# Identity products in spare PSUM columns while TensorE waits in the first batch's attention

## The chip, the cores and the metric

The kernel runs on one core of a Trainium2 chip. A core has a matrix engine (TensorE, PE in the rows below, with a weight loader PEld beside it), VectorE (DVE), ScalarE (ACT), GpSimd (POOL) and SyncE (SP), which issues the transfers. Each engine takes its instructions in the order of the program, and semaphores make one wait for another. The metric is the device time of one execution in microseconds.

## The reference

Pooled attention over 8 batches of 8 heads feeds a gated feed-forward layer.

```python
def _attn_ref(q, k, v) -> np.ndarray:
    B, H, S, D = q.shape                      # 8, 8, 576, 64
    pool = 8
    Sp = S // pool
    scale = 1.0 / np.sqrt(D)
    k_p = k.reshape(B, H, Sp, pool, D).mean(axis=3)
    v_p = v.reshape(B, H, Sp, pool, D).mean(axis=3)
    scores = scale * np.matmul(q, k_p.transpose(0, 1, 3, 2))
    scores = scores - np.max(scores, axis=-1, keepdims=True)
    attn = np.exp(scores)
    attn = attn / (np.sum(attn, axis=-1, keepdims=True) + 1e-09)
    return np.matmul(attn, v_p).astype(np.float32)
...
def _moe_ref(x, w_gate, w_val, w_out, rms_g) -> np.ndarray:   # x: 4608 x 512, hidden width 1536
    rms = np.sqrt(np.mean(x * x, axis=-1, keepdims=True) + 1e-06)
    xn = x / rms * rms_g
    g = xn @ w_gate
    silu = g * (1.0 / (1.0 + np.exp(-g)))
    val = xn @ w_val
    return (silu * val @ w_out).astype(np.float32)
```

## The kernel before

The attention works on one batch and one pair of heads at a time: batch 0 has the pairs 0 to 3. The feed-forward layer works on blocks of 512 tokens. Its first block needs all four pairs of batch 0 and most of its weights, which VectorE, ScalarE and GpSimd first split into a high and a low part. From the third block on, the products are formed by a scheme with seven products in place of eight. So the program starts with a short stretch in which all engines prepare, some 60 us, and then TensorE has feed-forward products to the end.

The order of the work is written out by hand in the long string `ORDER` (line 52). Each word of it is a step, and `run` (line 1109) calls the steps in that order; an engine's own order is the order in which the steps issue to it. Digits behind a colon name the PSUM banks that a step takes. A bank holds 128 x 512 numbers; there are eight, and a step that takes a bank waits for the readers of what stood in it. A leading `_` marks a step of batch 0, of batch 1's first pairs or of the first feed-forward block.

The steps that matter here, with batch b, pair p and half h or u (`_M021` is batch 0, pair 2, half 1):

- `K`, `V`: VectorE pools the keys and the values (lines 410, 419).
- `S` (`s_heads`, line 470): TensorE's scores, ten products into two banks, of which 5 x 72 = 360 columns are used. `M` takes the maxima and `U` subtracts them on VectorE (lines 428, 448), `E` and `O` make exponentials on ScalarE (lines 441, 453), `N` normalises on GpSimd (line 468).
- `T` (`s_pt`, line 525): TensorE transposes the weights, `C` and `D` copy them out on VectorE and ScalarE (lines 542, 544). Step `T` with half 2 uses 256 columns of its bank.
- `A` (`s_av`, line 545): weights times values, 288 columns. `Y`, `x` and `Z` read the result on ScalarE (lines 583, 1017, 590; `Z` squares it), `y` on VectorE (line 1023).
- `P` (`s_tokens`, line 637): TensorE sums the squares by products with a column of ones (line 652, tile psr). `p`, `r`, `s` make the reciprocal root, `B` spreads it (line 676, tile psb), `m` are the first gate products (line 1049, tile psg).
- `z` (`warm`, line 1170): products of the identity with itself. There is one such step, `_zg`, the first of all: 16 products.

An fp32 product shows as two MATMUL rows in the trace, a transpose as one.

Of the kernel before, what the change touches and what calls it, by code (L numbers as in the profile page):

```python
# [53 lines left out]
_k01 _O021 _K01 _f _k03 _v03 _V03 _I021 _K03 _R000 _O001 _q01 _I001 _h5 _N000 _N001 _S01:10 _M010 _k10 _M011 _U011
_E020 _N021 _R020 _K10/1 _N020 _q03 _S03:56 _M030 _E010 _l1 _R010 _W5 _M031 _N010 _q10 _O011 _T000:3 _I011 _N011 _E030
_v02 _D000 _l0 _a1/1 _a0/0 _V02 _R030 _S10:04 _M100 _l2 _U031 _T020:2 _E100 _l3/1 _b1 _c1 _N030 _T022:3 _D022 _b0 _d1
_O031 _c0 _h1 _W1 _a2 _R100 _T001:7 _d0 _T002:1 _D001 _D002 _T030:6 _D030 _T011 _I031 _N031 _M101 _a3/1 _T021:5 _D021
_C011 _E101 _N100 _T010:3 _T031 _v00 _V00 _A001:7/0 _Z01 _Y001 _x01 _D020 _b3 _b2 _c3 _c2 _d2 _h0 _y01 _T012:1 _W0
_A000:5 _Z00 _h2 _W2 _D012 _T032:6 _D010 _v01 _A020:4 _k11 _d3 _h3 _l4 _P00:2 _V01 _C032 _w3 _R101 _A021:1 _v10 _x20
_y20 _A010:3 _x00 _y00 _V10/0 _m000:7 _K11/1 _Y021 _x21 _y21 _Z21 _m010:6 _D031 _l7/0 _a7/1 _b7 _c7 _a4 _Z10 _ld/1 _l6  # L60
_ad/0 _m002 _b4 _Z20 _bd _A011:5 _Y011 _Z11 _d7 _x11 _A030 _x30 _Z30 _cd _c4 _x10 _dd _A031:4 _Z31 _P01 _P02 _P03 _a6
_hd _m012 _N101 _d4 _l9/0 _p _T100:1/1 _T101:2 _q11 _y30 _x31 _b6 _k12 _Wd _y11 _r0 _h7 _D101 _y31 _s0 _B00:5 _h4 _y10
_m011 _m001 _m013 _D100 _a9/0 _m003 _n _W4 _m100:5 Wt0/1 _l8 _Y031 _c6 _d6 _W7 _v11 _a8 _T102 _u0 _G0 _h6 _A100:1/1
_S11:27 _b9 _C102 _c9 _d9 _M110 _h9 _m102 _E110 _b8 _m110 _m112 _M111 _F0 _w9 _m101 _W6 _c8 _i0/1 _L0 Wf00 _d8 _lb/0
_R110 _m111 _K12/1 _A101:4 _ab/1 _X101 _bb _B01:6 _h8 _H01 _cb _m103 _u1 wf01 _db Wf02 _E111 _w8 _G1 _m113 _F1 wh03/0
Wl03 _la _X100 _hb _Wb _lf/0 Wf03 ws03 _e2:0 _o0:7564 _aa _g2:3 _i1/1 _ba _ca _L1 wh02/1 _o1 wl02 _af/0 _u2 _G2 _R111
_bf _cf _F2 _N110 _Q10 wd0 _i2/1 _T110:2/1 _D110 _df _hf _Wf _da _j2 _ha _g3:1 _lc _q12 _e3:0 wh01/0 _V11/0 _u3 _G3
_wa ws02 _o2 _N111 _F3 _ac _bc _cc _dc _k13 _i3/0 _lh/0 _ah/1 _hc _g4 _T112:1 _bh _D112 _j3 _T111:3 _le _D111 _e4:0
_ch _u4 _dh _hh wl01 ws01 Wt1/0 wh04/0 _ae Wl04 _Wc Wf10 _S12:32 _lg _Wh Wf11 Wf12 wf13 _be _M120 _M121 ws04 _G4 _F4
wh11/1 wl11 _ce _de _A110:1 _v20/1 _V20/1 _Y110 ws11 _o3 _A111:1 wh13/0 wd1 _i4/0 Wt2/1 _E120 _g5:0 wh14/1 _R120 Wl14  # L70
ws14 Wf20 _li Wl13 _L4 ws13 _ag _o4 _bg _e6 _he _We Wf21 _u5 _cg _E121 _R121 _dg wf22 _N121 wh12/1 Wl12 _e5:2 ws12 _G5
_Y111 _T121:1/1 Wf23 _F5 _i5/0 wh23/0 _v12 _j5 _N120 _D121 Wl23 wh21/1 Wl21 _q13 _K13/1 _T122 _ai _bi _ll/0 _hg ws23
ws21 _Wg _g6 _u6 _V12/0 _D122 _lk _k20 _v13 _o5 _G6 wh22/1 _F6 _i6/1 _ci _S13:10 _M130 _T120:3 _di wh24/0 Wl24 _D120
_j6 wl22 _M131 _g7 _u7 _hi ws22 _e7 _ak _o6 _K20/1 _bk _ck _G7 _F7 ws24 _E130 _dk _A121:3 _al/1 _bl _cl _ln/1 _an/0
_bn _cn _dl _i7/1 _R130 _dn _E131 _R131 _N131 _A120:2 _Y120 _hn _Wn _j7 _Y121 _g8:1 _u8 _V13/0 _G8 _wi _N130 wd4 _e8:0
_F8 _hl _wl _lj/0 _aj/0 _bj _cj _lm/1 _am/1 _bm _dj _T131:1/1 _o7 _D131 _hk _T130 _D130 _q20 sc20:21 wd2 _Q11/0 _cm
_T132 _D132 _dm _Wk _hj _A130:3 _Y130 Wt3/1 Wf30 _A131 _Y131 Wf31 lv21/0 mx201/1 sb201 _hm _Wj _wm _J11 mx200/1 lk21
# [1132 lines left out]
```

## Time and profile before

| | us |
|---|---|
| median of 3 runs | 975.91 (975.13 to 976.47) |
| the profiled execution, its own time | 976.88 |
| its span, first to last instruction | 975.1 |
| TensorE busy | 947.5 (97%) |
| VectorE, ScalarE, GpSimd busy | 704.2, 492.9, 490.4 |

The share of TensorE is that of the whole span. The stretch that the change touches is the first 60 us, where TensorE waits at places and where its granted clock changes several times; a view by short windows and the engines' timelines show that stretch.

### The profile page before, as it was taken

Reading aid. Unit: us, or ns where it says so; the run is one execution under the profiler, and the core shown is the slowest. Engines: PE = TensorE matmul, PEld = TensorE weight load, DVE = VectorE, ACT = ScalarE, POOL = GpSimd, SP = SyncE. Lnnn points to the kernel's source line nnn. Section 1 sums busy time; section 2 is a strip of 40 time slices with the busy share of each in tenths; the row PEclk is TensorE's granted clock in tenths of the full one; section 3 lists DMA queues with packets and bytes.
Section 4 is the critical chain, followed back from the end, with each engine's and each line's share of the span. In section 5 each row is a group of like instructions: output and inputs, shape, how many; then the busy total and the mean of one; then the engine's idle time right before and its main releaser. Section 6 shows DMA issues by size and latency. Waiting matters only on the chain.

```text
span 975.1 us, 14181 instructions
## 1 busy us (share of the span) xinstructions
PE 947.5 (97%) x4670; PEld 752.2 (77%) x4670; DVE 704.2 (72%) x1134; ACT 492.9 (51%) x929; POOL 490.4 (50%) x618
## 2 busy tenths in 40 slices
PE   7799999999999999999999999999999999999997
PEld 6577677777777877877877777877877778888885
DVE  6989898978787888778787877755565884433333
ACT  5876675645555647555455456242543642213332
POOL 3355637222322324433455788432296894445785
PEclk7789999999999999999999999999999999999999
DMA  9537774665766569878887776768686465767646
GB/s 300 183 137 273 225 247 157 215 204 178 240 204 204 171 182 267 251 231 274 253 248 255 202 253 195 243 184 263 217 257 212 155 219 173 229 189 232 205 141 204
DMA packets 142296, 211.41 MB, mean 217 GB/s; under 512 B 12240, under 2 KB 78288, under 8 KB 140944
## 3 DMA queue, kind: packets, MB, share of 16 engines
q1 hardware_dynamic: 142224, 210.52, 68.8%
...
HBM read 154.24 MB, written 56.23 MB: 216 GB/s over the span
## 4 chain that ended last, share of the span: by engine, by line
PE 76%; DMA 5%; DVE 5%; POOL 5%; ACT 3%; issue 2%; SPq 1%; DVEq 0%; ACTq 0%; POOLq 0%
PE pxy L895 30%; PE psg L1059 15%; PE pf L975 15%; PE po L1093 7%; PE psx L560 3%; PE pss L478 3%; POOL w L292 2%; DMA pt<-rows 1%; DMA ring<-vs 1%; POOL xp L292 1%; POOL hl L292 1%; DMA ring<-vB 1%; DVE wt L326 1%; PE psr L652 1%; DVE wt L330 1%
## 5 line engine op out<-in xcount | busy, mean ns | idle before, releaser
L895 PE MATMUL pxy<-xp,wp 128*128 128x512 f32 x1512 | 361.1, 391 | 1.5 <-ACT o L1104 0.7
L895 PEld LDWEIGHTS pxy<-xp,wp 128*128 128x128 f32 x1512 | 282.3, 188 | 65.3 <-issue 2.5
L975 PE MATMUL pf<-fp,ring 128*128 128x512 f32 x756 | 189.8, 393 | 3.1 <-DMA ring<-vB 1.6
L1059 PE MATMUL psg<-xh,w 128*128 128x512 f32 x544 | 171.2, 396 | 1.4 <-DVE prob L495 1.0
L975 PEld LDWEIGHTS pf<-fp,ring 128*128 128x128 f32 x756 | 139.6, 188 | 39.6 <-DMA ring<-vs 3.9
L1059 PEld LDWEIGHTS psg<-xh,w 128*128 128x128 f32 x544 | 101.2, 189 | 26.5 <-DVE prob L495 1.4
L1059 PE MATMUL psg<-xl,w 128*128 128x512 f32 x272 | 106.7, 392 | 0.0
L292 POOL TENSOR_TENSOR hl<-act,hh 128x256 fp32r<-128x256 f32 x58 | 49.8, 878 | 111.5 <-ACT hh L1075 102.6
L292 POOL TENSOR_TENSOR fp<-fs,fp 128x256 fp32r<-128x256 f32 x108 | 81.1, 778 | 41.7 <-ACT fp L948 37.9
L292 POOL TENSOR_TENSOR fp<-act,fp 128x256 fp32r<-128x256 f32 x72 | 55.1, 786 | 83.1 <-ACT fp L948 81.8
L1093 PE MATMUL po<-w,hh 128*128 128x512 f32 x288 | 72.9, 390 | 0.0
L292 POOL TENSOR_TENSOR w<-wt,w 128x256 fp32r<-128x256 f32 x50 | 48.7, 1000 | 45.7 <-ACT w L344 45.7
L1093 PEld LDWEIGHTS po<-w,hh 128*128 128x128 f32 x288 | 54.1, 188 | 11.6
L292 POOL TENSOR_TENSOR fp<-hb,fp 128x256 fp32r<-128x256 f32 x68 | 54.5, 828 | 13.9 <-ACT fp L948 13.9
L1059 PEld LDWEIGHTS psg<-xl,w 128*128 128x128 f32 x272 | 51.4, 189 | 11.1
L1154 ACT COPY hb<-pxy 128x512 f32<-128x512 f32 x36 | 21.0, 586 | 72.7 <-PE pxy L895 72.7
L1161 DVE TENSOR_TENSOR u<-u,pxy 128x512 f32<-128x512 f32 x36 | 24.7, 685 | 38.0 <-PE pxy L895 37.8
L948 ACT CAST fp<-act 128x512 fp32r<-128x512 f32 x36 | 22.2, 619 | 58.5 <-DVE act L1162 49.3
L948 ACT CAST fp<-fs 128x512 fp32r<-128x512 f32 x54 | 33.0, 618 | 34.3 <-POOL fs L292 16.7
L1155 DVE TENSOR_TENSOR u<-hb,pxy 128x512 f32<-128x512 f32 x36 | 24.6, 684 | 33.3 <-PE pxy L895 19.7
L292 POOL TENSOR_TENSOR fs<-act,hb 128x256 f32<-128x256 f32 x32 | 23.4, 752 | 50.0 <-DVE act L1162 28.0
L1158 DVE TENSOR_TENSOR hb<-u,pxy 128x512 f32<-128x512 f32 x36 | 24.7, 686 | 29.0 <-PE pxy L895 28.1
...
## 6 DMA issues: line engine op xcount, KB each, us to landing
wp<-sum SPq DMA_DIRECT2D x144, 256.0 KB
wp<-blocks SPq DMA_DIRECT2D x108, 256.0 KB
...
```

The costliest lines, as they stand in the source:

```text
L292: getattr(eng, op)(*(x[..., o:o + step] for x in (out, a, b)))
L478: nc.tensor.matmul(s["ps", h][:, t * SP:(t + 1) * SP], s["q"][r, o:o + P], s["pk"][r, :], start=True, stop=True)
L560: nc.tensor.matmul(ps[r, :n], s["pv"][:, r], x, start=True, stop=True)
L895: nc.tensor.matmul(ps[:, :NB], w[:, a, c, :], x[:, b, c, :], start=j == 0 and not more, stop=j == len(todo) - 1, skip_group_check=more)
L948: nc.scalar.copy(y[:, 0], f_source(i, k, j))
L975: nc.tensor.matmul(ps[c], w[:, a, c * P:(c + 1) * P], x[:, b], start=j == 0 and n == 0 and not more, stop=j == HALF - 1 and n == 2, skip_g ...
L1059: nc.tensor.matmul(ps[:, :NB], w[:, c, cols], x[c], start=(j == 0), stop=(j == len(todo) - 1))
L1093: nc.tensor.matmul(po[i][t], x[i, f][:, t * P:(t + 1) * P], w, start=(f == 0 and k == 0), stop=(f == NF - 1 and k == 2))
L1154: cp=lambda i, f: S_.copy(later(i, f), st["XY", i, f, 0]),
L1155: u2=lambda i, f: V.tensor_add(u2(i, f), later(i, f), st["XY", i, f, 1]),
L1158: c2=lambda i, f: V.tensor_sub(later(i, f), u3(i, f), st["XY", i, f, 4]),
L1161: v1=lambda i, f: V.tensor_add(u2(i, f), u2(i, f), st["XY", i, f, 5]),
```

## The change

Five steps `_z` with 10, 4, 9, 7 and 3 products are put between the steps of batch 0, and the first one grows from 16 products to 22 (`_zg` to `_zm`, the count is in base 36) and takes bank 1 in place of bank 6. All other steps keep their order. The new ones have no bank of their own: the list `spare` holds the last 128 columns of a bank that `S`, `T` (half 2) or `A` has just taken, which those steps leave unused.

```diff
@@ ORDER, the lines with a new step @@
-_zg:6 _q00 _q02 _l5/0 _k00 _K00 _S00:16 _a5/0 _b5 _c5 _k02 _K02 _S02:24 _M001 _M000 _U001 _E000 _d5 _M021 _M020 _U021
...
+_zm:1 _q00 _q02 _l5/0 _k00 _K00 _S00:16 _a5/0 _b5 _c5 _k02 _K02 _S02:24 _M001 _M000 _U001 _E000 _d5 _M021 _M020 _U021
+_k01 _O021 _K01 _f _k03 _v03 _V03 _I021 _K03 _R000 _O001 _q01 _I001 _h5 _N000 _N001 _za _S01:10 _M010 _k10 _M011 _U011
+_E020 _N021 _R020 _K10/1 _N020 _q03 _S03:56 _M030 _E010 _l1 _R010 _W5 _M031 _N010 _q10 _O011 _z4 _T000:3 _I011 _N011
...
@@ s_heads @@
         for h in (0, 1):
             s["ps", h] = bank(0, f"pss{b}_{p}_{h}")
+        spare[:] = [s["ps", 1][:, 512 - P:]]
@@ s_pt @@
         ps = s["pst", h] = bank(0, f"pst{b}_{p}_{h}")
+        if h == 2:
+            spare[:] = [ps[:, 512 - P:]]
@@ s_av @@
         ps = s["psx", u] = bank(0, f"psx{b}_{p}_{u}")
+        spare[:] = [ps[:, 512 - P:]]
@@ warm @@
-        ps = bank(0, "warm")
+        ps = spare[0] if spare else bank(0, "warm")[:, 512 - P:]
         for _ in range(n):
-            nc.tensor.matmul(ps[:, :P], ident, ident, start=True, stop=True)
+            nc.tensor.matmul(ps, ident, ident, start=True, stop=True)
```

`_z9` stands between `_T010` and `_T031`, `_z7` between `_D010 _v01` and `_A020`, `_z3` between `_dd` and `_A031`.

TensorE between the scores of pair 2 and those of pair 1, before. The names are tile, batch, pair and half; in brackets stand the engines or transfer queues whose semaphore the row waits for.

```order
L478 MATMUL pss0_2_0_138<-own2_136,main2_111 128x72
L478 MATMUL pss0_2_1_139<-own2_136,main2_111 128x72
L478 MATMUL pss0_1_0_190<-own1_168,main1_164 128x72 [waits DMAHW1_49,DVE_49,Activation_49]
L478 MATMUL pss0_1_1_191<-own1_168,main1_164 128x72
L478 MATMUL pss0_1_0_190<-own1_168,main1_164 128x72
```

The same place after the change:

```order
L480 MATMUL pss0_2_0_144<-own2_142,main2_117 128x72
L480 MATMUL pss0_2_1_145<-own2_142,main2_117 128x72
L1179 MATMUL pss0_2_1_145<-ident_69 128x128 [waits DVE_49]
L1179 MATMUL pss0_2_1_145<-ident_69 128x128 x9
L480 MATMUL pss0_1_0_206<-own1_174,main1_170 128x72 [waits DMAHW1_49,DVE_49,Activation_49]
L480 MATMUL pss0_1_1_207<-own1_174,main1_170 128x72
```

Ten identity products now stand ahead of pair 1's scores, and the first waits for VectorE: its semaphore value is that of `_U021`, the last instruction of VectorE that reads the tile pss0_2_1.

TensorE between the last scores of pair 3 and the first of batch 1, before:

```order
L478 MATMUL pss0_3_1_221<-own3_176,main3_171 128x72
L536 MATMUL pst0_0_0_250<-ident_69,main0_108 72x128 [waits Pool_49]
L536 MATMUL pst0_0_0_250<-ident_69,main0_108 72x128 x3
L478 MATMUL pss1_0_0_275<-pk1_0_216,q1_0_247 128x72 [waits DMAHW5_49,DVE_49,PE_49]
L478 MATMUL pss1_0_1_276<-pk1_0_216,q1_0_247 128x72
```

And after:

```order
L480 MATMUL pss0_3_1_237<-own3_182,main3_177 128x72
L1179 MATMUL pss0_3_1_237<-ident_69 128x128 [waits DVE_49]
L1179 MATMUL pss0_3_1_237<-ident_69 128x128 x3
L540 MATMUL pst0_0_0_270<-ident_69,main0_114 72x128 [waits Pool_49]
L540 MATMUL pst0_0_0_270<-ident_69,main0_114 72x128 x3
L480 MATMUL pss1_0_0_295<-pk1_0_232,q1_0_263 128x72 [waits DMAHW5_49,PE_49]
```

Four products and a wait for VectorE (for `_M031`, the last reader of pss0_3_1 that is issued ahead of them) now stand ahead of the transposes `_T000` and of batch 1's scores `_S10`.

TensorE around the last product of weights and values of batch 0, before:

```order
L560 MATMUL psx0_1_1_490<-own1_168 64x288 x2
L560 MATMUL psx0_3_0_498<-own3_176 64x288 [waits Activation_49]
L560 MATMUL psx0_3_0_498<-own3_176 64x288
L560 MATMUL psx0_3_1_508<-own3_176 64x288 [waits PE_49,Activation_49]
L560 MATMUL psx0_3_1_508<-own3_176 64x288
L652 MATMUL psr0_428<-one_74,own1_168 128x1 x2
```

And after:

```order
L565 MATMUL psx0_1_1_526<-own1_174 64x288 x2
L565 MATMUL psx0_3_0_534<-own3_182 64x288 [waits Activation_49]
L565 MATMUL psx0_3_0_534<-own3_182 64x288
L1179 MATMUL psx0_3_0_534<-ident_69 128x128 [waits Activation_49]
L1179 MATMUL psx0_3_0_534<-ident_69 128x128 x2
L565 MATMUL psx0_3_1_547<-own3_182 64x288 [waits PE_49]
L565 MATMUL psx0_3_1_547<-own3_182 64x288
L657 MATMUL psr0_464<-one_74,own1_174 128x1 x5
```

Three products stand ahead of `_A031`. They wait for ScalarE's `_Z30`, the square that reads psx0_3_0; before, `_A031` waited for the older square `_Z20`, which had read the bank that `_A031` takes.

## Rows read from the trace of the kernel before

**Rows 1.** The head of the profile's page and its line of busy times.

```profile
span 975.1 us, 14181 instructions
PE 947.5 (97%) x4670; PEld 752.2 (77%) x4670; DVE 704.2 (72%) x1134; ACT 492.9 (51%) x929; POOL 490.4 (50%) x618
```

**Rows 2.** The chain of work that ended last, in order of time, around the sums of squares: start us, us, what.

```profile
40.52 0.37 DVE xl L1023
...
41.22 0.57 ACT own L542
...
44.30 0.31 ACT own L590
...
44.65 0.71 PE psx L560 x4
45.36 6.01 PE psr L652 x30
51.37 1.49 PE psg L1049 x3
52.86 1.71 PE pst L536 x8
54.57 1.84 PE psb L676 x10
```

**Rows 3.** TensorE's timeline: start us, us, engine, line, operation, tile, count, and in brackets the idle time before it with what ended it.

```profile
1.47 5.46 PE L1174 MATMUL warm<-ident 128*128 128x128 f32 x32 [1.47 <-POOL ident masks.py:199]
...
10.69 1.51 PE L478 MATMUL pss<-own,main 64*128 64x72 f32 x20 [0.38 <-DVE own L410]
14.63 4.79 PE L478 MATMUL pss<-own,main 64*128 64x72 f32 x40 [2.43 <-DVE own L410]
19.35 1.07 PE L536 MATMUL pst<-ident,main 128*72 128x128 f32 x4
20.34 2.41 PE L478 MATMUL pss<-pk,q 64*128 64x72 f32 x20
...
26.19 1.50 PE L536 MATMUL pst<-ident,main 128*72 128x128 f32 x12 [0.28 <-ACT prob L441]
29.83 0.63 PE L536 MATMUL pst<-ident,main 128*72 128x128 f32 x4 [2.13 <-POOL main L468]
...
34.07 0.71 PE L560 MATMUL psx<-own 72*64 72x288 f32 x4 [1.65 <-ACT own L542]
...
42.64 1.19 PE L560 MATMUL psx<-own 72*64 72x288 f32 x8
44.65 0.71 PE L560 MATMUL psx<-own 72*64 72x288 f32 x4 [0.82 <-ACT own L590]
45.29 6.08 PE L652 MATMUL psr<-one,own 128*128 128x1 f32 x30
```

**Rows 4.** Windows of 1 us in which the granted clock changes: the window, its length, busy us (and instructions) of PE, PEld, DVE, ACT and POOL, then the clock (1.00 is 2.4 GHz, 0.50 is 1.2 GHz, between them the mean of both), the DMA share and GB/s.

```profile
11.00:12.00 1.00, 1.00 (x20) 0.99 (x16) 1.00 (x4) 0.42 (x2) 0.00 (x0) 0.86 1.04 363
...
25.00:26.00 1.00, 0.91 (x7) 0.58 (x5) 1.00 (x4) 1.00 (x8) 0.00 (x0) 0.82 0.47 122
...
35.00:36.00 1.00, 1.00 (x8) 1.00 (x9) 1.00 (x2) 1.00 (x3) 1.00 (x2) 0.80 0.00 0
...
42.00:43.00 1.00, 1.00 (x6) 0.38 (x7) 0.58 (x2) 1.00 (x2) 0.00 (x0) 0.78 0.02 8
...
45.00:46.00 1.00, 1.00 (x10) 0.71 (x6) 1.00 (x3) 1.00 (x5) 0.00 (x0) 0.92 0.00 0
...
56.00:57.00 1.00, 1.00 (x7) 0.87 (x6) 0.97 (x2) 1.00 (x3) 0.79 (x1) 0.96 0.00 0
```

**Rows 5.** Windows that count the rows of line 1174 alone (the opening identity products); a row that began before the window counts too. Columns: window, length, busy us (and rows) of PE and PEld, clock, DMA share, GB/s.

```profile
2.00:4.50 2.50, 2.50 (x14) 2.50 (x13) 1.00 0.90 267
5.00:6.50 1.50, 1.50 (x16) 1.50 (x15) 1.00 0.98 321
2.00:2.01 0.01, 0.01 (x2) 0.01 (x1) 1.00 0.11 4
...
5.00:5.01 0.01, 0.01 (x3) 0.01 (x2) 1.00 5.72 1638
```

**Rows 6.** VectorE's timeline: `_U021`, then `_M010` with `_M011`, `_M031`, and the first maxima of batch 1, `_M100`.

```profile
13.35 0.52 DVE L448 TENSOR_TENSOR main<-pss,early 128x360 f32<-128x360 f32 x1
...
17.59 0.94 DVE L428 TENSOR_REDUCE early<-pss 128x5 f32<-128x360 f32 x2
...
20.45 0.49 DVE L428 TENSOR_REDUCE early<-pss 128x5 f32<-128x360 f32 x1
...
22.92 0.49 DVE L428 TENSOR_REDUCE early<-pss 128x5 f32<-128x360 f32 x1
...
30.28 1.12 DVE L322 TENSOR_SCALAR wt<-wt 128x512 uint32<-128x512 uint32 x2 [0.21 <-ACT wt L318]
```

**Rows 7.** ScalarE's timeline: `_D002`, the square `_Z01`, the square `_Z30`.

```profile
28.93 0.26 ACT L544 COPY own<-pst 72x128 f32<-72x128 f32 x1
...
32.72 0.39 ACT L590 ACTIVATE own<-psx 128x288 f32<-128x288 f32 x1
...
45.55 0.48 ACT L590 ACTIVATE own<-psx 128x288 f32<-128x288 f32 x1
```

**Rows 8.** The rest of the span in one window, columns as in rows 4.

```profile
60.00:975.00 915.00, 898.82 (x4380) 713.04 (x4379) 658.34 (x1048) 449.89 (x796) 468.54 (x583) 1.00 0.69 216
```

More of the change, by code (lines that the diff above doesn't have):

```diff
@@ L52 @@
 ORDER = """
-_zg:6 _q00 _q02 _l5/0 _k00 _K00 _S00:16 _a5/0 _b5 _c5 _k02 _K02 _S02:24 _M001 _M000 _U001 _E000 _d5 _M021 _M020 _U021
[L54 to L77, printed above, removed]
@@ new lines @@
+_E030 _v02 _D000 _l0 _a1/1 _a0/0 _V02 _R030 _S10:04 _M100 _l2 _U031 _T020:2 _E100 _l3/1 _b1 _c1 _N030 _T022:3 _D022
+_b0 _d1 _O031 _c0 _h1 _W1 _a2 _R100 _T001:7 _d0 _T002:1 _D001 _D002 _T030:6 _D030 _T011 _I031 _N031 _M101 _a3/1
+_T021:5 _D021 _C011 _E101 _N100 _T010:3 _z9 _T031 _v00 _V00 _A001:7/0 _Z01 _Y001 _x01 _D020 _b3 _b2 _c3 _c2 _d2 _h0
+_y01 _T012:1 _W0 _A000:5 _Z00 _h2 _W2 _D012 _T032:6 _D010 _v01 _z7 _A020:4 _k11 _d3 _h3 _l4 _P00:2 _V01 _C032 _w3
+_R101 _A021:1 _v10 _x20 _y20 _A010:3 _x00 _y00 _V10/0 _m000:7 _K11/1 _Y021 _x21 _y21 _Z21 _m010:6 _D031 _l7/0 _a7/1
@@ new lines @@
+_b7 _c7 _a4 _Z10 _ld/1 _l6 _ad/0 _m002 _b4 _Z20 _bd _A011:5 _Y011 _Z11 _d7 _x11 _A030 _x30 _Z30 _cd _c4 _x10 _dd _z3
+_A031:4 _Z31 _P01 _P02 _P03 _a6 _hd _m012 _N101 _d4 _l9/0 _p _T100:1/1 _T101:2 _q11 _y30 _x31 _b6 _k12 _Wd _y11 _r0
+_h7 _D101 _y31 _s0 _B00:5 _h4 _y10 _m011 _m001 _m013 _D100 _a9/0 _m003 _n _W4 _m100:5 Wt0/1 _l8 _Y031 _c6 _d6 _W7 _v11
+_a8 _T102 _u0 _G0 _h6 _A100:1/1 _S11:27 _b9 _C102 _c9 _d9 _M110 _h9 _m102 _E110 _b8 _m110 _m112 _M111 _F0 _w9 _m101
+_W6 _c8 _i0/1 _L0 Wf00 _d8 _lb/0 _R110 _m111 _K12/1 _A101:4 _ab/1 _X101 _bb _B01:6 _h8 _H01 _cb _m103 _u1 wf01 _db
@@ new lines @@
+_bp _La _s1 _B11:1 wd5 _cp _dp _hp _ub _Gb _H11 wt4/0 _B10 _H10 _wp _eb:2 dm20 _Fb _oa sc21:10 wf40 wh41/0 Wl41 _t0
+ws41 _t1 _ib/1 _jb wf41 wh43/1 _ob lk22 Wl43 _t2 ws43 _t3 dp20/0 me10:2 Zt00/1 mg10:3 ev03/0 Wf42 Zt01 Zf00 Zf01
+zh03/1 mx210/0 st03 sb210 Zl03 pk22/1 mx211/1 ev00/0 zs03 Zf02 Wf43 sb211 ex210 sm210/1 lq22 kt1 zh02/1 Zl02 ex211
+sm211/1 st00 Nm210 zs02 wh42/0 Wl42 Nm211 av200:4/1 xc200 ws42 ev02/1 st02 me12:1 sc22:47 gt10 vl10 wh44/0 Wl44 hi10/0
+lk23 ev01/1 mx221/1 ws44 st01 tr21/0 mx220/0 sb220 sb221 Lo10 mg11:6 Zf03 gt11 me11:0 dm21 vl11 zh04/0 zh01/1
@@ new lines @@
+dp23/1 xc220 sq22/1 ex301 Jn22 mx300/0 pk31/0 mo13 hi14/1 lv30/1 sb300 Wf62 Lo14 wh61/0 Wl61 ws61 wh63/1 Wl63 ws63
+wf63 mg15:0 gt15 sm301/0 nm301 lk32 ex300 me15 pv30/1 av231:2 xc231 wh64/0 sm300/0 Nm300 Wl64 av230:1 mo14 wh62/1 Wl62
+lv31/1 ws64 xc230 vl15 tr30/0 hi15/0 Lo15 pk32/1 lq31 mg16:0 pv31/0 gt16 Zt10/1 ws62 Zf10 zh11/0 zl11 Zt11 Zf11 Zf12
+me16:1 zh13/1 xd23 mo15 Zl13 dm30 vl16 sc31:20 mx310/0 zs11 sb310 zs13 mg17:1 hi16/1 Lo16 dp30/1 zh12/1 Zf13 zh14/0
+mx311/0 mo16 sb311 zd4 gt17 Zl12 Zl14 Wt7/0 Wf70 zs14 Wf71 Wf72 wf73 sq23/1 Jn23 zs12 me17 ex310 av300:1/0 wh72/0
@@ new lines @@
+sm310/1 ex311 sm311/0 wh71/1 Wl71 xc300 lq32 zd1 vl17 hi17/1 Nm310 wl72 ws72 ws71 wh73/0 sh2/0 wh74/1 Nm311 tr31/1
+sc32:02 mx320/0 sb320 av301:3 xd30 Lo17 dm31 ex320 xc301 Wl73 mx321/1 Wl74 Wt8/0 sb321 Wf80 mg18:1 ws73 gt18 Wf81 lk40
+Wf82 ws74 wh81/0 mo17 Sl2 rm21:3 rt21 Wf83 wh84/1 Wl81 wl84 ws81 sm320/0 me18:2 vl18 dp31/1 rm20 rt20 hi18/1 Lo18
+pk40/0 ws84 lv33/1 rc21 rs21 wh82/0 Wl82 mg19:1 gt19 wh83/1 me19:2 av310:1 vl19 ex321 sm321/1 xc310 wl83 av311:3 lk33
+xc311 mo18 hi19/0 pv33/0 pk33/1 xd31 lv32/0 ws82 pv32/1 Zt20/0 Lo19 Zt21 Zf20 mg1a gt1a Nm321 Zf21 Zf22 zh22/0 Nm320
@@ new lines @@
+ev12/1 Jn31 av331:6 xc331 xd33 ev13/0 sq32/0 jn32 st12 Wfa0 wda Wfa1 gt21 av330:5 xc330 mg22:1 mo20:6745 st13 ex401
+sq33/0 Jn33 sh3/0 vl21 pk41/0 lv41/0 hi21/0 lo21 me22:0 mo21 Sl3 Wfa2 wha2/0 Wla2 rm30:2 wha1/1 Wla1 ex400 sm401/1
+wfa3 gt22 vl22 hi22/1 Lo22 wd3 rt30 wsa1 pv41/0 Nm401 rc30 rs30 wsa2 wha4/1 Wla4 me23 lk42 wha3/0 Wla3 mg23:1 pk42/1
+rm31:2 Zt30/1 zt31 mo22 lv40/0 gt23 vl23 pv40/1 me24:0 rt31 hi23/1 mg24:1 kt2 sm400/1 wsa3 Nm400 Lo23 tr40/0 Zf30 wsa4
+zh31/1 Zf31 lq41 sc41:23 mx411/1 Zl31 sb411 dm40 zs31 ft300 Zf32 zh33/0 Zl33 zs33 mo23 gt24 vl24 ex411 me25 Zf33
@@ new lines @@
+zt40/1 Nm430 zt41 vl27 Nm431 me28:0 mo26 dm42 sq40 lq50 tr43/0 wsb2 hi27/1 wsb4 Zf40 Zf41 Lo27 zh41/1 Zl41 ft311
+dp42/1 Zf42 Zf43 mg28:3 sc50:12 mx501/1 dm43 zh43/0 gt28 vl28 zl43 zs43 sb501 yh31 zs41 yl31 mx500/1 sq41/0 jn41 mo27
+zh42/0 Zl42 hi28/0 zh44/1 Zl44 sb500 mg29:0 dp43/0 av430:3 ex501 lk51 pk51/0 av431:1 xc430 wd9 xd43 av421:2 xd42 xc431
+wd7 zt50/0 Zt51 sm501/0 av420:3 xc420 me29:1 Lo28 ex500 xc421 zs44 sq42/1 Jn42 Zf50 gt29 vl29 zs42 zd5 sq43/1 Jn43
+mo28 sm500/1 hi29/1 yh30 yl30 Nm501 sh4/0 Lo29 Zf51 me2a zh53/1 Nm500 wd8 Zf52 zh52/0 lq51 Sl4 wd6 mg2a:1 Zl53 tr50/1
@@ new lines @@
+gt2a vl2a rm40:2 rt40 hi2a/0 mo29 dm50 rc40 Lo2a rs40 yh32 ys33 Zf53 ys34 me2b:2 zs53 mg2b:3 yh33 rl300/4 Yl33 rl303/5
+gt2b rl310/7 sc51:10 mx510/0 vl2b Zl52 mo2a hi2b/1 mx511/1 pr300:3 cp30 rl320/6 rl312/0 zs52 Lo2b ys35 yh35 zh54/1
+pr310 rl315/3 Zl54 cp31 mo2b pr312 lk52 pk52/0 rl304/1 yh34 Yl34 rl302/4 ev22/0 pr302 rl321/2 lv50/1 sb511 sa31 ex511
+st22 zs54 yl32 Yl35 pr320:0 pr304:4 ev21/0 pr315:7 rl301/7 sb510 sa30 rl311/4 sm511/0 pv50/0 ev20/1 rl313/6 ex510
+rl314/0 sm510/0 Nm510 pr301:6 u230 st21 st20 ev23/0 ys36 pr303 u330 pr313:1 c230 pr311:5 rl305/1 pr305:6 yh36 zh51/1
@@ L353, in body @@
     given = []
+    spare = []
     def bank(k, name):
```

86 lines of the change are left out of this document (34 added, 52 removed).

## The prediction

> **What bounds the kernel now.** I read the busy line first [rows 1]: TensorE works 947.5 of 975.1 us, so whatever moves the moment at which its long stretch of products begins moves the end. Then the window from 60 us on [rows 8]: 898.8 of 915 us busy, 16 us idle in all, and what it waits for there is fed by products of the same stretch. So I take a shift at 60 us to arrive at the end whole. What decides is the path to 60 us.
>
> The chain of waits shows that path [rows 2]: up to 40.9 us VectorE (the product low part `_y21`), then ScalarE (copies, weights and squares) to 44.6, then TensorE alone: `_A031`, the sums of squares for 6.01 us, then 1.49 + 1.71 + 1.84 us. Before 40 us TensorE is not on it: its waits are for VectorE, GpSimd or ScalarE [rows 3], while VectorE waited 0.21 us at 30.28 [rows 6] and otherwise ran instruction behind instruction from 8 to 40 us. There a faster TensorE buys nothing, and a later one costs once VectorE has to wait for it.
>
> The clock [rows 4]: it falls to 1.2 GHz at about 11.7 us, right in the scores of pair 2, rises at 25.4, falls at 35.6, rises at 42.4, falls at 45.8 when the sums of squares have just begun, and rises at 56.1. Half clock on the path is therefore only the stretch from 45.8 to 56.1 us.
>
> **The cost of one dummy.** In the opening run 14 rows less the 2 begun earlier start in 2.5 us: 0.21 us a row. Later 16 less 3 start in 1.5 us: 0.115 us [rows 5]. The clock column says 1.00 in both, but the spacing halves, so I read the first as 1.2 GHz and the second as 2.4. A product is two rows: 0.42 us at half, 0.23 at full.
>
> **Part by part.**
>
> `_zm`: 12 more rows, 1.4 us, in the 2.04 us that TensorE waits before 8.96 anyway (the opening run ends at 6.93 [rows 3]). Cost 0. The bank it takes changes nobody's wait.
>
> `_za`: 20 rows. They wait for `_U021`, which ends at 13.87 [rows 6]; TensorE was idle from 12.2 and could have started pair 1's scores at 14.63 [rows 3]. From 13.97 the 20 rows take 2.3 us all at full, 4.2 all at half. The clock stands at half there, and the opening run needed some 16 rows before its spacing halved; I take 14 at half and 6 at full, 3.6 us, to 17.6. The scores behind them (20 rows, 1.34 us at full, 2.4 at half) then end at 18.9 instead of 17.0. `_M010` stood at 17.59 on VectorE: it now starts at 19.0, 1.4 us late (bounds 0 and 2.9).
>
> `_z4`: it waits for `_M031`, which ended at 20.94 and now ends at 22.3. Before, `_T000` started at 19.35 and `_S10` at 20.34, with no gap for a dummy [rows 3]. Eight rows take 0.9 or 1.7 us; I take half clock, since plain scores let the clock fall at 11.7 [rows 4]: to 24.1. `_T000` 1.07 to 25.1, `_S10` at full 1.34 to 26.4 (at half 2.41). `_M100` stood at 22.92 on VectorE and had no reserve: it comes 3.5 us late. All at full it would be 0.9 late, all at half 6.1. Behind `_M100` on VectorE stand the weight splits and everything up to `_y21`; the only reserve is the 0.21 us at 30.28 [rows 6]. I carry 3.3 us to 40.9, and so to ScalarE's squares.
>
> `_z9`, counted without the shift that all engines share by then: 18 rows, 2.1 us at full, after `_D002`, which ended at 29.19 [rows 7]. `_T031` comes at 31.3 instead of 29.83, and the product for `_Z01` at about 32.6 against the 32.72 at which ScalarE gets there: covered by ScalarE's queue, barely; at half clock up to 1.0 us uncovered. `_z7`: 14 rows, 1.6 us, in the 1.65 us before 34.07 [rows 3], pushed by `_z9`; ScalarE's backlog covers it. Cost 0 for both.
>
> `_z3`: it waits for `_Z30`, which ended at 46.03 [rows 7]; `_A031` had started at 44.65, after `_Z20` [rows 2, 3]. Six rows take 0.7 us (1.25 at half), `_A031` 0.64. The sums of squares then begin at 47.4 instead of 45.29, 2.1 us late (3.1 at half).
>
> What the clock gives back: the 30 rows of the sums took 6.08 us, nearly all at half. If their spacing halves as the dummies' did, 3.3 us: 2.8 saved. The 5.04 us behind them [rows 2] would save 2.5. [...] I take half of the sums at full, 1.3 saved, and 0.5 on the rest.
>
> Sum: 3.3 + 2.1 - 1.3 - 0.5 = 3.6 us later. On the profiled execution's 976.88 that is 980.5; the median of the runs lies 0.97 below the profiled one, so 979.5.
>
> The wait of each dummy is what hurts, and the order shows it although the dummies' columns are not read by anybody. By column alone `_za` could start at 12.3 and end before 16, `_z4` would fill nothing but a short gap, and `_z3` would fit in the 0.82 us before 44.65; the sum would be about 3 us faster. The trace of before has no such pair. The Trainium skill, "PSUM — Partial Sum Buffer", section "PSUM bank collisions raise a hardware error", says that engines have to be kept apart by bank and group of partitions, not by address, disjoint columns included. That speaks for the waits as the order has them, and against filling a gap that begins before the bank's readers are done; the sum above goes by the order.
>
> **The rivals.**
>
> A, the clock stays at 2.4 GHz from the first dummies to 56 us. For it: all gaps are filled, the longest left are under 2 us. Against it: it fell at 11.7 us in the midst of scores [rows 4], which nothing new keeps dense. Its price: `_M100` 0.9 late less 0.2, plus 2.1, less 2.8, less 2.5: 2.5 us faster, 973.4. The Trainium skill's "TensorE: Matmul & The Clock Gate", section "Why this matters for your kernels", asks for just this, TensorE without long gaps between bursts, to keep the clock; that fall at 11.7 behind a wait of 0.38 us [rows 3] shows that short gaps were not enough here.
>
> B, the delay stands but `_z3` and its neighbours carry the clock through the sums and beyond: 3.3 + 2.1 - 2.8 - 2.0 = 0.6 later, 976.5. For it: the clock was full at 45 us before, with less work around it. Against: it fell at 45.8 nevertheless.
>
> C, the dummies run at half clock throughout: 6.1 - 0.2 + 1.0 + 3.1 with nothing given back, 10 us, 986. It decides if 20 rows at 13.97 do not raise the clock before pair 3's scores. Against it: the opening run raised it with about as many.
>
> D, the changed clock falls elsewhere, with no net delay: VectorE's lateness would have to be absorbed before 40 us, by a reserve that I do not see in its timeline. Then A's gains stand without the 0.7: about 973.
>
> **How the numbers follow.** Forecast 0.52, A 0.11, B 0.23, C 0.10, D 0.04. Two executions of this kernel tell about 0.2%, 2 us, from no change. Faster is most of A and all of D: 0.13. Same is B, a rest of A and the lower edge of the forecast: 0.27. Slower is the forecast's bulk and C: 0.60. The range leaves out the far ends of A, D and C: 974.0 to 983.5; the forecast's own is 977.5 to 982.
>
> **What would show it.** In the profile after: the row of ten dummies behind a wait for line 449 on VectorE, starting near 14 us and ending after 16.5; `_S01` behind it later than 14.63; a wait of VectorE before `_M010` or `_M100` for TensorE's scores, which it never had; the sums of squares starting some 5 us later than 45.29 and taking less than 6 us. Wrong would be: a clock of 1.00 in every window from 12 to 56 us, VectorE without waits at its maxima, or a first `_A031` before 46 us.

## The result and the profile after

| | before | after |
|---|---|---|
| median of 4 runs each, us | 976.19 (975.13 to 977.37) | 984.93 (982.58 to 985.35) |
| the profiled execution, its own time | 976.88 | 985.35 |
| its span | 975.1 | 983.6 |

The ratio of the medians is 1.0079, 95% interval 1.0056 to 1.0102: the change costs 8.7 us, more than the forecast's 3.6 and more than its range.

The head of the page of after:

```profile
span 983.6 us, 14335 instructions
PE 956.0 (97%) x4748; PEld 760.5 (77%) x4748; DVE 704.7 (72%) x1134; ACT 493.3 (50%) x929; POOL 492.2 (50%) x618
```

TensorE is busy 8.5 us more in a span that is 8.5 us longer, with the same 97% as in [rows 1]. The share says nothing of the loss: the 78 new rows count as work like any other.

The long stretch, with its window moved by the 8.74 us by which it starts later (see below), columns as in [rows 4]:

```profile
68.74:983.58 914.84, 898.43 (x4384) 711.94 (x4382) 659.76 (x1049) 450.07 (x796) 470.31 (x583) 1.00 0.70 216
```

TensorE is idle for 16.4 us of it, against 16.2 in [rows 8]: in these two executions the long stretch takes nothing and gives nothing back. So the loss has to arise ahead of it. The chain of waits there, columns as in [rows 2]:

```profile
13.73 4.63 PE pss L1179 x20
...
23.11 2.08 PE pss L1179 x8
...
50.46 0.31 ACT own L595
...
50.81 1.65 PE psx L1179 x6
...
53.62 6.49 PE psr L657 x30
60.12 1.49 PE psg L1054 x3
61.60 1.71 PE pst L540 x8
```

From 50 us on it is the chain of [rows 2], ScalarE's squares and then TensorE alone, with one new link: the dummies of `_z3` (psx, line 1179). Further ahead it now runs through `_za` and `_z4` (pss, line 1179); in before it can be followed back to 26.62 us, and TensorE is not on it until 44.65. TensorE's timeline, columns as in [rows 3]:

```profile
13.73 4.63 PE L1179 MATMUL pss<-ident 128*128 128x128 f32 x20 [1.72 <-DVE main L449]
18.30 2.46 PE L480 MATMUL pss<-own,main 64*128 64x72 f32 x40
23.11 2.08 PE L1179 MATMUL pss<-ident 128*128 128x128 f32 x8 [2.36 <-DVE early L429]
...
25.98 2.41 PE L480 MATMUL pss<-pk,q 64*128 64x72 f32 x20
...
34.01 2.27 PE L1179 MATMUL pst<-ident 128*128 128x128 f32 x18 [0.67 <-ACT own L548]
...
38.51 1.73 PE L1179 MATMUL pst<-ident 128*128 128x128 f32 x14
...
50.81 1.65 PE L1179 MATMUL psx<-ident 128*128 128x128 f32 x6 [3.48 <-ACT own L595]
52.40 1.23 PE L565 MATMUL psx<-own 72*64 72x288 f32 x4
53.55 6.56 PE L657 MATMUL psr<-one,own 128*128 128x1 f32 x30
```

All five groups stand where the order put them, four of them behind a wait for a reader of their bank: `_za` for `_U021` (line 449), `_z4` for `_M031` (line 429), `_z9` for `_D002` (line 548) and `_z3` for `_Z30` (line 595). The wait of `_z9` holds up nobody: ScalarE comes to `_Z01`, the square behind it, at 37.49 without idle time. VectorE's timeline shows who pays for the first two: `_M010` with `_M011`, `_M031`, `_M100`, the low part `_y21`, and the reduction that follows the sums of squares:

```profile
19.66 0.97 DVE L429 TENSOR_REDUCE early<-pss 128x5 f32<-128x360 f32 x2 [2.18 <-PE pss L480]
...
22.57 0.49 DVE L429 TENSOR_REDUCE early<-pss 128x5 f32<-128x360 f32 x1
...
28.42 0.53 DVE L429 TENSOR_REDUCE early<-pss 128x5 f32<-128x360 f32 x1 [3.29 <-PE pss L480]
...
45.23 0.43 DVE L1028 SCALAR_TENSOR_TENSOR xl<-psx,gmean,xh 128x224 fp32r<-128x224 f32 x1
...
60.15 0.18 DVE L662 TENSOR_REDUCE total<-psr 128x5 f32<-128x20 f32 x1 [6.58 <-PE psr L657]
```

The two waits for TensorE's scores in brackets are new. `_M010` is 2.07 us later than in [rows 6], `_M100` 5.50, and `_y21`, which stood at 40.44 before, 4.79. The last row is a good marker for the whole of the stretch, since the chain of waits runs through the sums that it follows. In before it stood here:

```profile
51.41 0.18 DVE L657 TENSOR_REDUCE total<-psr 128x5 f32<-128x20 f32 x1 [2.57 <-PE psr L652]
```

That is 8.74 us later. The medians differ by 8.74 and the two profiled executions by 8.47, so all of the loss is there by 60 us. ScalarE's `_Z30`, which `_z3` waits for, is late by what VectorE is late:

```profile
50.34 0.43 ACT L595 ACTIVATE own<-psx 128x288 f32<-128x288 f32 x1
```

Windows of 1 us in which the granted clock changes, columns as in [rows 4]:

```profile
18.00:19.00 1.00, 1.00 (x14) 0.78 (x15) 0.00 (x0) 0.00 (x0) 1.00 (x2) 0.84 1.07 426
21.00:22.00 1.00, 0.00 (x0) 0.00 (x0) 1.00 (x4) 1.00 (x8) 0.62 (x1) 0.87 0.76 307
...
49.00:50.00 1.00, 0.00 (x0) 0.00 (x0) 0.93 (x2) 1.00 (x6) 0.00 (x0) 0.52 0.00 0
66.00:67.00 1.00, 1.00 (x5) 0.77 (x5) 0.09 (x1) 1.00 (x3) 1.00 (x2) 0.94 0.00 0
```

The column of the clock turns into moments by its mean: 0.84 is full for the last 68% of its window. So the clock rises at 18.3 us, as the ten products of `_za` end, and falls at 21.7 in the wait of `_z4` (PE busy 0.00 in that window). It rises once more at 32.0 and falls at 49.0, in the 3.48 us in which `_z3` waits. From there to 66.1 us TensorE runs at 1.2 GHz, all thirty rows of the sums included.

So the loss has three parts: 4.79 us by which VectorE is late; 3.47 us between VectorE's lateness and the start of the sums (they begin 8.26 later than in [rows 3]: 1.37 because `_z3` waits for `_Z30` where `_A031` had waited for `_Z20`, 1.59 until its six rows let `_A031` start, and 0.51 because `_A031` runs at half clock); and 0.48 us in the sums, which take 6.56 in place of 6.08.

### The profile page after: what moved, and what is told of

It reads as the page before. It is cut to its first block, busy times and chain, and to the rows that moved or that the text cites. A ratio compares the mean times of both kernels' runs of the same rounds, so it can differ in the third digit from the quotient of the medians.

```text
span 983.6 us, 14335 instructions
## 1 busy us (share of the span) xinstructions
PE 956.0 (97%) x4748; PEld 760.5 (77%) x4748; DVE 704.7 (72%) x1134; ACT 493.3 (50%) x929; POOL 492.2 (50%) x618
## 4 chain that ended last, share of the span: by engine, by line
PE 74%; POOL 7%; DVE 6%; ACT 5%; DMA 4%; issue 2%; SPq 1%; ACTq 0%; DVEq 0%; POOLq 0%
PE pxy L900 31%; PE pf L980 14%; PE psg L1064 14%; PE po L1098 7%; PE pss L480 3%; PE psx L565 3%; POOL fp L292 2%; POOL w L292 2%; POOL xp L292 1%; DMA wp<-blocks 1%; DMA wx<-w 1%; DVE wt L330 1%; DMA pt<-rows 1%; POOL hl L292 1%; ACT wt L318 1%
## 5 line engine op out<-in xcount | busy, mean ns | idle before, releaser
L292 POOL TENSOR_TENSOR hl<-act,hh 128x256 fp32r<-128x256 f32 x58 | 49.8, 880 | 111.4 <-ACT hh L1080 102.4
L292 POOL TENSOR_TENSOR fp<-hb,fp 128x256 fp32r<-128x256 f32 x68 | 54.5, 830 | 13.7 <-ACT fp L953 13.7
```

Of the source, the lines that this page charges most:

```text
L292: getattr(eng, op)(*(x[..., o:o + step] for x in (out, a, b)))
```

## The experiments

Theory: the time goes to the waits for readers of a bank, which put TensorE's own later work behind VectorE and ScalarE, and to the clock that falls in those waits. Rival 1: it goes to the dummies' own length (20, 8 and 6 rows in the way). Rival 2: it comes from a clock that the other dummies (`_zm`, `_z9`, `_z7`) have moved; all kernels but fill_alone have these three. In the table the marker is the start of VectorE's reduction of the sums, 51.41 in before.

| kernel | marker, us | against before | median, us | before, same set of runs | ratio, 95% interval |
|---|---|---|---|---|---|
| after | 60.15 | +8.74 | 984.93 | 976.19 | 1.0079 (1.0056 to 1.0102) |
| no_last | 55.81 | +4.40 | 982.73 | 977.13 | 1.0074 (1.0051 to 1.0097) |
| only_last | 55.57 | +4.16 | 982.60 | 977.13 | 1.0064 (1.0035 to 1.0092) |
| outer | 52.68 | +1.27 | 979.07 | 977.13 | 1.0025 (1.0003 to 1.0047) |
| free_banks | 50.92 | -0.49 | 976.53 | 977.13 | 1.0000 (0.9981 to 1.0019) |
| one_each | 56.10 | +4.69 | 983.64 | 976.78 | 1.0071 (1.0058 to 1.0084) |
| fill_wait | 48.83 | -2.58 | 975.86 | 976.78 | 0.9989 (0.9974 to 1.0003) |
| fill_sums | 53.33 | +1.92 | 977.16 | 976.78 | 1.0010 (0.9994 to 1.0025) |
| fill_alone | 51.60 | +0.19 | 977.81 | 977.17 | 1.0010 (0.9995 to 1.0025) |
| fill_two | 49.99 | -1.42 | 976.40 | 977.17 | 0.9993 (0.9976 to 1.0011) |

Executions of one kernel spread over up to 7.5 us here (before: 973.4 to 980.9 in one set), so single differences below 2 us are read with their intervals.

The marker is that of one execution, and two things limit it. It counts from the start of the span, and VectorE's first pooling, which waits for the first keys, starts between 7.94 and 9.05 us (8.15 in before): that alone is 0.9 us of the marker in fill_sums and 0.3 in outer, fill_alone and fill_two. And it says nothing of what comes later. VectorE has the same instructions in the same order in all kernels, so their starts can be compared with those of before to the end. After stays 7.1 to 9.4 us late all the way. The profiled execution of outer goes from 1.3 us late at the marker to 6.1 at the end, that of fill_alone from 0.2 to 3.2, and that of fill_wait from 2.6 us early to 2.7 late; in outer, fill_wait and fill_sums it is the longest execution of its set. No run shows that these later losses come from the dummies, so effects on the time are read from the medians.

### Without the last dummies: no_last

```diff
-_x10 _dd _z3 _A031:4
+_x10 _dd _A031:4
```

> The changed kernel without the last block of three products ahead of the last weights-times-values product of batch 0. Theory W (a block costs by its wait for the readers of its bank, and the costs of the places add): the 4.8 us that VectorE is late at its low part of pair 2 stay, the 3.5 us ahead of the sums of squares go; the sums begin near 50 us instead of 53.55 and the time is 4.8 to 5.5 us over before, 981 to 981.7. Theory C (what costs is the half clock alone, wherever it falls): the clock still falls in the wait there, so little changes, 983.5 to 985.

Measured: +5.6 us. TensorE's timeline:

```profile
48.13 1.16 PE L565 MATMUL psx<-own 72*64 72x288 f32 x4 [2.06 <-ACT own L595]
49.22 6.56 PE L657 MATMUL psr<-one,own 128*128 128x1 f32 x30
```

The first half of the theory stands: `_za` and `_z4` alone make VectorE's `_M100` wait 2.11 us, and `_y21` comes at 43.97, 3.5 us late. But the sums stay at half clock without `_z3` too: `_A031` waits 2.06 us here, against 0.82 in [rows 3], and the clock falls at 48.3, as that wait ends. The sums begin at 49.22, near the 50 of the forecast. Its 4.8 to 5.5 us over before (981 to 981.7) was missed by 0.1 us as a difference and by 1.0 as a time.

### Only the last dummies: only_last

```diff
-_N000 _N001 _za _S01:10
+_N000 _N001 _S01:10
...
-_q10 _O011 _z4 _T000:3
+_q10 _O011 _T000:3
```

> The changed kernel without the blocks of ten and four products between the scores; the last block stays. Theory W: VectorE keeps its times of before, its low part of pair 2 at 40.4 us; the last block starts after the square of pair 3, near 46.1, and the sums of squares begin near 49 us instead of 45.3: 3.5 to 4.5 us over before, 979.7 to 980.7. Theory C: VectorE's lateness was only a follower of the clock, so the same half clock from 46 us on leaves 7 us or more, 983.

Measured: +5.5 us. TensorE's timeline:

```profile
46.23 1.65 PE L1179 MATMUL psx<-ident 128*128 128x128 f32 x6 [2.69 <-ACT own L595]
...
48.97 6.56 PE L657 MATMUL psr<-one,own 128*128 128x1 f32 x30
```

VectorE is as before here (`_y21` at 40.62, `_M100` at 23.09), and still the sums begin 3.7 us later than in [rows 3]. `_z3` waits 2.69 us for `_Z30` with the queue behind it, the clock falls in that wait, and from the start of the six rows to the sums it takes 2.7 us, in place of the 1.3 that the prediction's full clock gives. The forecast, 3.5 to 4.5 us over before (979.7 to 980.7), was missed by 1.0 us as a difference and by 1.9 as a time.

### Neither: outer

```diff
-_N000 _N001 _za _S01:10
+_N000 _N001 _S01:10
...
-_q10 _O011 _z4 _T000:3
+_q10 _O011 _T000:3
...
-_x10 _dd _z3 _A031:4
+_x10 _dd _A031:4
```

> Only the longer opening block and the blocks of nine and seven products are left. Theory W: they lie in waits that TensorE has anyway, within 1 us of before, 975.2 to 977.2; the clock of 1.00 that they hold from 25 to 42 us buys nothing, since TensorE is not on the path there. Rival: holding the clock in that stretch is worth something, 973 to 974; or their waits push the products behind them and it costs 1.5 us or more.

Measured: +1.9 us, with an interval that leaves out no change, if barely; the 975.2 to 977.2 of the theory is missed, and the rival's 1.5 us or more came. TensorE's timeline, then the window in which the clock falls:

```profile
44.93 1.23 PE L565 MATMUL psx<-own 72*64 72x288 f32 x4 [2.06 <-ACT own L595]
46.08 6.56 PE L657 MATMUL psr<-one,own 128*128 128x1 f32 x30
```

```profile
44.00:45.00 1.00, 0.07 (x2) 0.08 (x4) 0.86 (x3) 1.00 (x5) 0.00 (x0) 0.63 0.00 0
```

Rival 2 has a share. In this execution the clock, with `_z9` and `_z7` in TensorE's waits, stays up through the first gate products, so TensorE is through earlier and waits 2.06 us for ScalarE where it had waited 0.82 [rows 3]. In that longer wait the clock falls, and `_A031` and the sums run at half from their start. In before, TensorE came to this place at half clock, which rose at 42.4, and it had the first rows of the sums at full. Being early at a wait was worth less here than being late with the clock up. Of the marker's 1.27 us this is 1.0, and 0.3 is the later load. That `_z9` and `_z7` hold the clock is not sure: it fell amid the gate products in two of the nine profiles with them, at 39.0 in only_last and 40.3 in one_each. No run takes one of the three steps out alone.

The shares add up: no_last less outer is 3.7 us, only_last less outer 3.5, outer itself 1.9; together 9.1 against the 8.7 measured. By the marker it is 3.1 + 2.9 + 1.3 = 7.3. Whether the two places also act on each other is not shown: the two counts miss 8.7 on either side, and the interval of outer alone is 4 us wide.

### The same dummies in banks that nobody reads: free_banks

```diff
-_za _S01:10
+_za:7 _S01:10
...
-_z4 _T000:3
+_z4:7 _T000:3
...
-_z3 _A031:4
+_z3:1 _A031:4
...
-        ps = spare[0] if spare else bank(0, "warm")[:, 512 - P:]
+        ps = spare[0] if spare and not given else bank(0, "warm")[:, 512 - P:]
```

> The changed kernel with the blocks of ten, four and three products written to banks that nobody reads at the time (7, 7 and 1), so that none waits for VectorE or ScalarE; as many products as in the change. Theory W: the block of ten starts near 12.2 instead of 13.7 and ends near 16.6, VectorE's first maxima of pair 1 come 1 to 1.5 us late, the block of four costs nothing more, the last block fits in the wait ahead of it; 0 to 2 us over before less what the clock gives back: 974.5 to 978. Rival O (the dummies' own time is what costs, not their waits): 981 or more.

Measured: no difference to before (0.9981 to 1.0019). This decides against rival 1: the same 34 rows at the same three places, without the waits. TensorE's timeline, then VectorE's `_M010` and `_M100`:

```profile
11.74 2.50 PE L1179 MATMUL warm<-ident 128*128 128x128 f32 x20
14.64 1.34 PE L480 MATMUL pss<-own,main 64*128 64x72 f32 x20 [0.40 <-ACT main L454]
...
43.06 0.94 PE L1179 MATMUL warm<-ident 128*128 128x128 f32 x6
45.21 0.71 PE L565 MATMUL psx<-own 72*64 72x288 f32 x4 [1.21 <-ACT own L595]
45.85 5.03 PE L657 MATMUL psr<-one,own 128*128 128x1 f32 x30
```

```profile
17.60 0.93 DVE L429 TENSOR_REDUCE early<-pss 128x5 f32<-128x360 f32 x2
...
24.26 0.54 DVE L429 TENSOR_REDUCE early<-pss 128x5 f32<-128x360 f32 x1 [1.24 <-PE pss L480]
```

`_za` starts 2 us earlier and ends before pair 1's scores can begin; `_M010` is where it was [rows 6]. Only `_z4`, which never had a gap (its rows take 2.07 us between `_S03` and `_T000`, which followed each other before), makes `_M100` wait 1.24. The shorter sums pay for that: the clock holds until 47.6, and they take 5.03 us.

### One product each behind the same waits: one_each

```diff
-_za _S01:10
+_z1 _S01:10
...
-_z4 _T000:3
+_z1 _T000:3
...
-_z3 _A031:4
+_z1 _A031:4
```

> The changed kernel with one product each in place of ten, four and three, in the same banks: the waits for the readers stay, the products' own time (0.2 to 0.4 us a place) all but goes. Theory W (the waits cost): pair 1's scores are not delayed, the scores of batch 1 come after the last maxima of pair 3, so VectorE waits there for 1.5 to 3 us; the last block still waits for the square of pair 3 and the sums begin at 48 to 51 us; 5 to 7 us over before, 982 to 984. Theory O (the products' own time): 1 to 2 us over before, about the time of the run that keeps only the outer blocks, 978 to 979.

Measured: +6.9 us with 6 rows in place of 34, inside the theory's 5 to 7. TensorE's timeline and VectorE's `_M100`:

```profile
21.17 0.80 PE L1179 MATMUL pss<-ident 128*128 128x128 f32 x2 [1.59 <-DVE early L429]
...
47.62 0.79 PE L1179 MATMUL psx<-ident 128*128 128x128 f32 x2 [2.73 <-ACT own L595]
...
49.50 6.56 PE L657 MATMUL psr<-one,own 128*128 128x1 f32 x30
```

```profile
25.20 0.53 DVE L429 TENSOR_REDUCE early<-pss 128x5 f32<-128x360 f32 x1 [2.01 <-PE pss L480]
```

`_za` with one product costs `_M010` nothing (17.76). At `_z4` the wait with two rows makes `_M100` 2.3 us late, of which 1.6 are left at `_y21`; with the wait at `_z3` the sums begin at 49.50, all at half clock. The kernel has `_zm`, `_z9` and `_z7` as well, so the share of outer has to come off. By the marker 1.3 of the 8.7 us are outer's, 3.4 come with the three waits and 4.0 with the 28 further rows, which raise `_M100`'s delay from 2.3 to 5.5 us; by the medians it is 1.9, 4.9 and 1.9. So rival 1 has a share, where rows stand behind a wait; free_banks shows that the same rows, where they need not wait, cost nothing on balance.

### Filling the gap that the clock falls in: fill_wait

Without `_za` and `_z4`; in place of `_z3`, eight products in bank 1, which no engine reads any more.

```diff
-_x10 _dd _z3 _A031:4
+_x10 _dd _z8:1 _A031:4
```

> The outer blocks, and eight products in bank 1, which nobody reads any more, ahead of the last weights-times-values product, in place of the three that wait; none between the scores. Theory W with the clock: the eight products lie in TensorE's wait of about 2 us there and end before 45, so the sums begin at full clock near 45.5 and take 5 us or less in place of 6.1 to 6.6: 1 to 3 us under the run with the outer blocks alone, 974 to 977.5. Rival (the sums let the clock fall whatever stands ahead of them, and the rest is at half as before): no difference from before beyond 1 us, or, where the products end too late, 1 us over.

Measured: 0.9 us less than before, with an interval that includes no change (0.9974 to 1.0003). TensorE's timeline:

```profile
42.47 2.05 PE L1179 MATMUL warm<-ident 128*128 128x128 f32 x16
...
45.28 3.51 PE L657 MATMUL psr<-one,own 128*128 128x1 f32 x30
```

The gap is full, the clock holds, and the thirty rows take 3.51 us against the 6.08 of [rows 3]: the marker comes 2.6 us earlier. Most of it does not reach the end. In the same profile TensorE then stands 2.47 us before line 1098, in a wait that was 1.48 in before, and the clock falls at 70.3, as it ends:

```profile
70.20 1.95 PE L1098 MATMUL po<-w,hl 128*128 128x512 f32 x4 [2.47 <-ACT prob L442]
```

That is only part of it. By VectorE's instructions the lead is 2.1 us behind that place, 0.9 at 200 us and gone by 450. Why, no run shows.

### Dummies between the sums: fill_sums

As fill_wait, with three products after each of `_P01` and `_P02`.

```diff
-_Z31 _P01 _P02 _P03
+_Z31 _P01 _z3:1 _P02 _z3:1 _P03
```

> As the run before, and three products more after the sums of pair 1 and after those of pair 2, in bank 1. If dense products keep the clock at 2.4 GHz through the sums, the sums with the six products take 4.6 us and what follows 2.6 in place of 5.0: the first scaled gate product comes 3 to 4 us earlier than before, 971.5 to 974. Rival: the clock falls within the sums all the same, the six products cost 1.4 to 2.5 us and it is 977 or more.

Measured: +0.4 us, interval 0.9994 to 1.0025; the 971.5 to 974 is missed and the rival's 977 or more came. TensorE's timeline:

```profile
47.37 0.91 PE L1179 MATMUL warm<-ident 128*128 128x128 f32 x6
48.12 1.76 PE L657 MATMUL psr<-one,own 128*128 128x1 f32 x10
49.74 1.63 PE L1179 MATMUL warm<-ident 128*128 128x128 f32 x6
```

The second dummies take 1.63 us against 0.91 for the first: the clock falls at 48.5 all the same, and the twelve rows are then pure cost on the path. Of the marker's 1.92 us, 0.9 is the later load of the keys.

### The one useful dummy alone: fill_alone

The kernel before with `_z8:1` ahead of `_A031`, none elsewhere.

```diff
-_x10 _dd _A031:4
+_x10 _dd _z8:1 _A031:4
```

> The kernel before with one thing added: eight identity products in bank 1 ahead of `_A031` (the step `_z8:1`), none elsewhere. Theory (what helps is that TensorE does not stand still ahead of the sums of squares, and the other dummies are not needed for it): the clock, which here rises at 42.4 us as before, stays up through `_A031`, the 30 sums take 3.5 to 5 us in place of 6.08, and the products behind them begin 1 to 3 us earlier; the time is 973 to 976, the same as or below that of fill_wait. Rival (the clock needs `_z9` and `_z7` ahead, which held it up to 42 us): the clock falls inside the sums again, they take some 6 us, and the time is that of the kernel before within 1 us.

Measured: +0.6 us, interval 0.9995 to 1.0025; the theory's 973 to 976 is missed. TensorE's timeline:

```profile
44.08 1.22 PE L565 MATMUL psx<-own 72*64 72x288 f32 x8
45.23 2.05 PE L1179 MATMUL warm<-ident 128*128 128x128 f32 x16
47.21 0.71 PE L565 MATMUL psx<-own 72*64 72x288 f32 x4
47.85 3.72 PE L657 MATMUL psr<-one,own 128*128 128x1 f32 x30
```

The sums are short (3.72), as the theory said, so `_z9` and `_z7` are not needed for that. But without them TensorE comes late: the products ahead end at 45.30 (44.08 and 1.22), ScalarE's square that `_A031` waits for had ended at 44.96, and so there was no gap. The dummies hold `_A031` back by their 1.9 us, the sums give back 2.4, and the marker ends within 0.2 us of before. A gap of 0.82 us in one execution is none in another; it takes 2 us of room for 2 us of dummies.

### The next gap too: fill_two

As fill_wait, with eight more products in bank 5 ahead of line 1098.

```diff
-_e2:0 _o0:7564
+_e2:0 _z8:5 _o0:7564
```

> fill_wait with eight more identity products in bank 5 (free since 66 us) in the wait ahead of `_o0:7564` at 67.8 to 70.2 us, behind which the clock fell in the profile of fill_wait and cost 1.3 us. Theory (idle time, not the kind of work, brings the clock down there): no fall at 69.7, the 12 rows of line 1098 that follow take 3.3 us in place of 4.4, and the lead over the kernel before at 100 us is 3 to 4 us in place of 2.4; the time is 973 to 975.5. Rival (identity products of 128 columns do not count for the clock as feed-forward products do, or the lead is eaten by the next wait for another engine): the fall comes at the same place or the lead at 150 us is no larger than in fill_wait, and the time is within 0.5 us of it.

Measured: 0.8 us less than before, interval 0.9976 to 1.0011, not to be told from fill_wait; the theory's 973 to 975.5 is missed. TensorE's timeline:

```profile
70.83 2.05 PE L1179 MATMUL warm<-ident 128*128 128x128 f32 x16 [1.27 <-DVE act L1038]
72.64 1.26 PE L1098 MATMUL po<-w,hl 128*128 128x512 f32 x4
```

The clock holds there, but bank 5 has a reader too (VectorE, line 1038): the dummies start only at 70.83, and ScalarE's last reading of bank 7, for which line 1098 had waited, was over at 70.3. The row of line 1098 starts 0.4 us later than in before, although the marker had been 1.4 us earlier. It is the mistake of `_z3` again, in small. The clock of these two executions also differs where their order is the same: the sums took 3.51 us in fill_wait and 4.30 in fill_two. Within the sums, the order alone does not set the moment of the fall.

## Why the prediction was wrong in size and right in kind

Its mechanism was right: slower, by waits for readers of banks whose columns the dummies don't share, with VectorE's first two waits in this stretch and a marker that arrives late. free_banks against after shows that directly. The time lies above its range because each step that leaned on the clock leaned the wrong way.

- `_zm`, `_z9`, `_z7`: "cost 0". As work in the way, yes. Not as a change of the clock: outer costs 1.9 us (0.3 to 4.6 by its interval), of which its profile shows 1.0, by the way through the wait before `_A031`. The prediction had looked for a cost only in time that they take, not in time that they win.
- `_za`: "14 at half and 6 at full, 3.6 us". It took 4.63; the clock rose only as they ended. The scores behind did run at full (40 rows in 2.46), and `_M010` came 2.07 us late, not 1.4, inside its bounds of 0 to 2.9.
- `_z4`: "half clock, to 24.1" and "`_S10` at full 1.34". The eight rows took 2.08 and ended at 25.2, and `_S10` took 2.41. The step that failed here is the clock of `_S10`, which the prediction had back at full behind `_z4`: it fell at 21.7 in `_z4`'s own wait of 2.36 us and stayed at 1.2 GHz until 32.0. `_M100` came 5.50 us late in place of 3.5, inside the bounds of 0.9 to 6.1; "I carry 3.3 us to 40.9" measured 4.79.
- `_z3`: "six rows take 0.7 us, `_A031` 0.64", the sums "2.1 us late (3.1 at half)". Beyond VectorE's lateness they were 3.47 late. The wait for `_Z30` in place of `_Z20` was sized right, 1.37 of it; the rows took 1.59 until `_A031` started, and `_A031` 1.15 until the sums. Half clock was the right end of the bound, and 0.4 short.
- "I take half of the sums at full, 1.3 saved, and 0.5 on the rest". This is the step that failed most. No row of after shows any of it: the sums took 6.56 us, all at half, and 1.49 and 1.71 stand behind them as in [rows 2]. (free_banks, where the rows need not wait, comes near the forecast half: 5.03.) What decided was the 3.48 us of idle time right ahead of the sums, in the wait that `_z3` itself brings, in which the clock fell at 49.0. That such a gap decides is what outer and fill_wait show, which differ only in the rows that fill it: 6.56 and 3.51 us for the same sums in one execution each, and 3.72 and 4.30 in fill_alone and fill_two. With the 0.48 that the sums lost this is the largest mis-sized term, 2.3 us; `_za` and `_z4` together are 1.5 and `_z3` 1.4.
- Sum: 3.3 + 2.1 - 1.8 = 3.6 predicted; 4.79 + 3.47 + 0.48 = 8.74 measured.

Rival C (half clock, nothing given back, 986) comes nearest in time, and most of its story held; its condition, that the twenty rows would not raise the clock before the next scores, did not. Rival A fell with the sums at half. In rival B `_z3` and its neighbours were to carry the clock through the sums: it fell in `_z3`'s own wait. Rival D fell with `_y21`: of `_M100`'s 5.50 us VectorE absorbed 0.71. Of the signs that the prediction named, the dummies' wait, the later `_S01` and VectorE's new waits came; the sums started 8.26 us late in place of some 5, and did not take less than 6.

"I take a shift at 60 us to arrive at the end whole" held for the loss: 8.74 at the marker, 8.74 in the medians. It did not hold for small differences: 2.6 us at the marker of fill_wait came to 0.9 in the median, and single executions drift by some 5 us behind the marker.

The rule of the Trainium skill that the prediction weighed ("PSUM — Partial Sum Buffer", section "PSUM bank collisions raise a hardware error") says to keep engines apart by bank, not by address. The rows of after agree as far as they go: `_za`, `_z4` and `_z3` wait 1.72, 2.36 and 3.48 us for readers of other columns of their bank. What would happen without those waits no run here shows.
